# A Fourier transform by real sums: the even-row half of each sequence transform split once more, by classes mod 4

## The chip, the cores and the metric

One core of a Trainium2 chip. The metric is the device time of one execution in microseconds (us). The kernel before takes 1970.43 us, the median of three runs from 1970.38 to 1970.59. The profiled execution has a span of 1969.1 us, with TensorE's granted clock at 0.999 of full speed.

## The reference

```python
X = np.fft.fft(x, axis=1)          # x: (8, 3008, 256), float32
X = np.fft.fft(X, axis=2)
a = X.real                          # -> (24064, 256)
h = a @ w_in                        # w_in: (256, 2048)
g = np.where(h > 0, h, np.exp(np.minimum(h, 0)) - 1)
out = g @ w_out                     # w_out: (2048, 256)
```

Only the real part of a two-dimensional transform is wanted, and then two matrix products with an ELU between them, for 24064 rows. The weights come as 64-bit floats and are turned to float32 on the chip.

## The kernel before

**Shape of the work.** The channel transform is folded into w_in once, at the start (`fold_chunk`, L399): this makes Wc and Ws, with which h is Wc times a cosine transform R plus Ws times a sine transform I of the sequence. A frequency k and its mirror 3008 - k share R and I, so only half of the frequencies, 1504 for each batch, are computed; h of the mirror comes by a subtraction (`h_minus`, L770). A tile holds 256 of these columns; there are 47 tiles of 8 slots each, 376 slots. A slot makes 256 of the 2048 hidden values for the tile's columns and their mirrors, and multiplies them with w_out.

**A slot.** TensorE runs P (`mm_P`: Wc times Rr, 2 matmuls), three products X1 of an earlier slot, Q (`mm_Q`: Ws times Ir, 2) and four products X2: eleven matmuls of 256 columns. X1 and X2 are seven products in place of eight (Winograd's way, from the third tile on); GpSimd makes the four sums they need (`sum_1`, `sum_3`, `sum_2`, `sum_4`, all through `gtt`, L391), of which sum_2 makes block 2, read by the third matmul of X1 (shown as pB<-G,WT). VectorE makes E (`even_part`, L764, between P and Q), h_minus (L774) and the two ELU results g_plus and g_minus (L790). ScalarE makes the exponentials (L394). At each tile's end VectorE recombines the products into u and v (L388), transposes them, and SyncE stores them.

**The sequence transform.** x of a batch is loaded in four sets of rows, L[0] to L[3]: rows counted up from 0, down from the end, down from the middle (1504), up from the middle. Partition p holds six successive rows, 6p to 6p + 5 (`load_x`, L150). L[0] and L[3] are plain transfers of 6 KB runs from SyncE. L[2] and L[1] run backwards and are gathered by GpSimd with a table of row numbers (`indirect_dma_start`, L157, one call each). `fold_x` adds and subtracts the sets, on GpSimd, two pieces to a tile from the slot's spare time, so that a transform needs only the rows 0 to 752. Then there are four transforms for each batch (class `Dft`, L567): cosine or sine (ri 0 or 1), even or odd frequencies (kodd 0 or 1), each 377 or 376 columns. Each of them is again two halves, over even rows s and over odd rows s: three matmuls of 377 columns accumulated in one PSUM bank (`dft_mms`, L536). Their sum and difference give two mirrored runs of frequencies:

```python
        def copy(self):                     # ScalarE: odd-row half, PSUM -> SBUF
            act(self.bs[0:M, 0:n], self.pb[0:M, 0:n])
        def plus(self):                     # VectorE, into the ring Rr or Ir
            vtt(self.ring[0:M, sl], self.bs[0:M, a:z], self.pa[0:M, a:z], ALU.add)
        def minus(self):
            vtt(self.ring[0:M, sl], u[0:M, o + a : o + z], v[0:M, o + a : o + z], ALU.subtract)
```

The odd-row half runs at the end of one slot (`at_half`, L1258: time 4.75 of the slot's 4.8), the even-row half two slots later. Batch 0 has its transforms at the start, some of them in banks pA to pD and M.

**The one channel that stands apart.** The channel at half the channel frequency has a transform of its own, R of channel 128, held in Rb. For batch 0 it is x_even (the first transform, `fold_first`) and `dft_ext_0`; for the others it is read with small strided loads (`load_ext`), passed through DRAM (`get_ext`, L633), folded (`fold_ext`), transformed for all batches at once (`dft_ext`, L666, four groups of 8 rows) and turned into rows by `ext_side` (ScalarE, L682) and `ext_rows` (L688; even frequencies on VectorE, odd ones on GpSimd).

**What sets the order.** Every instruction is put down with a time, `at(t, fn)`, in units of slots of T = 4.8; the list is sorted by it and pinned in that order on each engine, except transfers, which a scheduler may move. PSUM banks: tag H has three in turn (slots, transform halves, folds), pA to pD hold the products, M the mirror's exponentials.

Of the kernel before, what the change touches and what calls it, by code (L numbers as in the profile page):

```python
# [27 lines left out]
BW = 3 * NE  # L28
# [4 lines left out]
def _dft_consts():  # L33

    p = np.arange(128)
    out = np.zeros((128, 8, 3, NE), np.float64)
    n = 0
    for ri in range(2):
        fn = np.cos if ri == 0 else np.sin
        for kodd in range(2):  # L40
            k = 2 * np.arange(NE) + kodd
            for par in range(2):
                for t in range(3):
                    s = 6 * p + 2 * t + par
                    m = fn(2.0 * np.pi * ((s[:, None] * k[None, :]) % SEQ) / SEQ)
                    m[s > RUN] = 0.0
                    m[s == 0] *= 0.5
                    if ri == kodd:
                        m[s == RUN] *= 0.5
                    else:  # L50
                        m[s == RUN] = 0.0
                    out[:, n, t, :] = m
                n += 1
    return out.reshape(128, -1).astype(np.float32)
# [36 lines left out]
def kernel(  # L91
# [43 lines left out]
    def row_tables():  # L135


        for c, n, base in (
            (1, 128, HALF - 5),
            (0, 128, SEQ - 5),  # L140
            (2, 128, SEQ - 5),
            (2, 1, SEQ - 6),
        ):
            pin(
                nc.gpsimd.iota(
                    ix[0:n, c : c + 1], pattern=[[0, 1]], base=base, channel_multiplier=-6
                )
            )

    def load_x(b):  # L150
        L = [
            spool.tile([128, 6 * ND], FP, tag=f"xl{j}", bufs=1, name=f"xl{j}")
            for j in range(4)
        ]
        for j in (2, 1):
            c = 1 if j == 2 else 2 if b == NB - 1 else 0
            load = nc.gpsimd.indirect_dma_start(  # L157
                out=L[j],
                out_offset=None,
                in_=xflat,  # L160
                in_offset=bass.IndirectOffsetOnAxis(
                    ap=ix[:, c : c + 1].bitcast(U32), axis=0
                ),
                element_offset=b * SEQ * ND,
            )
            if b == 1:
                pin(load)
        nc.sync.dma_start(out=L[3], in_=xrows(b, HALF, 6, 128))
        nc.sync.dma_start(out=L[0], in_=xrows(b, 0, 6, 128))
        if b == NB - 1:  # L170
            nc.gpsimd.dma_start(
                out=L[1][0:1, 0 : 5 * ND], in_=xrows(b, SEQ - 5, 1, 1, 5)
            )
        return L
# [168 lines left out]
    for kodd in range(2):  # L343
        for ri in range(2):
            MC[ri, kodd] = cpool.tile(
                [128, 2 * BW], FP, tag=f"MC{ri}{kodd}", name=f"MC{ri}{kodd}"
            )

    def load_mats(ri, kodd, pieces=1):
        n = ri * 4 + kodd * 2  # L350
        w = 2 * BW // pieces
        for i in reversed(range(pieces)):
            nc.sync.dma_start(
                out=MC[ri, kodd][:, i * w : (i + 1) * w],
                in_=MC_dr.ap()[:, n * BW + i * w : n * BW + (i + 1) * w],
            )
# [178 lines left out]

    def dft_mms(ps, ri, kodd, par, stat, width):  # L536
        n = NO if kodd else NE
        for t in range(3):
            m = 2 * t + par
            c = par * BW + t * NE  # L540
            mm(
                ps[:, 0:n],
                stat[:, m * width : m * width + 128]
                if width > 1
                else stat[:, m : m + 1].to_broadcast([128, 128]),
                MC[ri, kodd][:, c : c + n],
                t == 0,
                t == 2,
            )
# [16 lines left out]

    class Dft:  # L567
# [7 lines left out]
        def mms(self, par, ps):  # L575
            dft_mms(ps, self.ri, self.kodd, par, self.stat, 1 if self.first else 128)
            if par:
                self.pb = ps
            else:
                self.pa = ps  # L580

        def copy(self):
            M, n = self.M, self.n
            self.bs = spool.tile([128, NE], FP, tag="bs", bufs=2, name="bs")
            act(self.bs[0:M, 0:n], self.pb[0:M, 0:n])

        def plus(self):
            M = self.M
            base = self.b * HALF + self.kodd * RUN
            for sl, a, z in ring_cut(base, self.n, False):  # L590
                vtt(self.ring[0:M, sl], self.bs[0:M, a:z], self.pa[0:M, a:z], ALU.add)

        def minus(self):
            M, n = self.M, self.n
            base = self.b * HALF + self.kodd * RUN
            u, v = (self.pa, self.bs) if self.ri == 0 else (self.bs, self.pa)
            o = 0 if self.kodd else 1
            m = n if self.kodd else n - 2
            top = base + RUN - 1
            for sl, a, z in ring_cut(top, m, True):  # L600
                vtt(self.ring[0:M, sl], u[0:M, o + a : o + z], v[0:M, o + a : o + z], ALU.subtract)
            if self.ri == 0 and not self.kodd and not self.first:
                vtt(R4[:, self.b : self.b + 1], u[:, 0:1], v[:, 0:1], ALU.subtract)
# [29 lines left out]
    def get_ext():  # L633
        xs = state["xs"] = spool.tile([128, 4, NB, 6], FP, tag="xs", bufs=1, name="xs")
        with nc.allow_non_contiguous_dma(reason="runs of six"):
            for j in range(4):
                nc.sync.dma_start(
                    out=xs[:, j], in_=xe_dr[j].rearrange("b (p m) -> p b m", m=6)
                )

# [8 lines left out]
    def dft_ext_0():  # L649

        ps = state["ext"] = bank("H")
        for t in range(3):
            for par in range(2):
                m, c = 2 * t + par, par * BW + t * NE
                g = 32 * (2 + par)
                mm(
                    ps[g : g + 1, 0:NO],
                    state["x_odd"][:, m : m + 1],
                    MC[0, 1][:, c : c + NO],
                    t == 0,  # L660
                    t == 2,
                )
# [3 lines left out]
    def dft_ext():  # L666

        xe = state["xe"]
        ps = state["ext"] = bank("H")
        for t in range(3):  # L670
            for g, (kodd, par) in enumerate(EXT):
                n = NO if kodd else NE
                c = par * BW + t * NE
                mm(
                    ps[32 * g : 32 * g + NB, 0:n],
                    xe[:, kodd, :, 2 * t + par],
                    MC[0, kodd][:, c : c + n],
                    t == 0,
                    t == 2,
                )  # L680

    def ext_side(g, rows=NB):  # L682
        n = NO if g > 1 else NE
        t = spool.tile([128, NE], FP, tag="bs", bufs=2, name="bs")
        act(t[0:rows, 0:n], state["ext"][32 * g : 32 * g + rows, 0:n])
        state["side", g] = t[0:rows, 0:n]

    def ext_rows(kodd, tt, rows=NB):  # L688
        n = NO if kodd else NE
        if not kodd or rows < NB:  # L690
            rx = spool.tile([128, HALF + 1], FP, tag="rx", bufs=1, name="rx")
            state["rx"] = rx[0:rows]
        if not kodd:
            a = state["ext"][0:NB, 0:n]
        else:
            a = state["side", 2]
        rx, b = state["rx"], state["side", 2 * kodd + 1]
        o, base = 1 - kodd, kodd * RUN
        m = n - 2 * o
        tt(rx[:, base : base + n], a, b, ALU.add)  # L700
# [359 lines left out]
    load_mats(0, 0, 2)  # L1060
# [50 lines left out]
    at(-13.0, lambda: dft_now(R_even, 1, "pA"))  # L1111
    at(-12.9, lambda: dft_now(R_even, 0, "pB"))

    at(-13.1, lambda: dft_now(state["x_even"], 1, "pC"))
    at(-13.1, lambda: dft_now(state["x_even"], 0, "pD"))
    at(-11.5, lambda: state["x_even"].copy())
    at(-11.0, lambda: fold_now("o0 o1 O0 EO2"))
    at(-10.95, R_even.copy)
    at(-10.9, R_even.plus)
# [6 lines left out]
    at(-10.5, lambda: dft_now(I_even, 1, "pC"))  # L1126
    at(-10.88, w1_chunks[1].round)
    at(0.05, lambda: dft_now(I_even, 0, "M"))
# [129 lines left out]
    def at_half(step, d, par, col):  # L1258
# [8 lines left out]
        if par:  # L1267
            at(t + T + 1.46, lambda: d().copy())
        else:
            at(t + T + 1.01, lambda: d().plus())  # L1270
            at(t + T + 1.02, lambda: d().minus())

    def at_dft(step, gap, b, ri, kodd, stat):
# [7 lines left out]
        at_half(step, d, 1, 0)  # L1281
        at_half(step + gap, d, 0, b * HALF + (kodd + 1) * RUN)
# [5 lines left out]
    for t, fn in (  # L1288
        (-1.8, I_even.copy),
        (0.6, I_even.plus),  # L1290
        (0.8, I_even.minus),
        (3.1, lambda: dft_now(R_odd, 1, "pA")),
        (3.2, lambda: dft_now(R_odd, 0, "pB")),
        (T + 2.6, R_odd.copy),
        (T + 4.2, R_odd.plus),
# [3 lines left out]
    at_half(3, lambda: I_odd, 1, 0)  # L1299
    at_half(5, lambda: I_odd, 0, HALF)  # L1300
# [11 lines left out]
    at(31.0 * T, get_ext)  # L1312
    at(32 * T + 1.35, fold_ext)
    at(32 * T + 4.75, dft_ext)
    at(33 * T + 1.46, lambda: ext_side(1))
    at(33 * T + 1.47, lambda: ext_side(2))
    at(34 * T + 0.99, lambda: ext_rows(0, vtt))
    at(34 * T + 1.46, lambda: ext_side(3))
# [83 lines left out]
```

## Time and profile before

| part of the page | figure |
|---|---|
| time, median of three | 1970.43 us |
| TensorE busy | 1956.1 us |
| VectorE busy | 1276.5 us |
| ScalarE busy | 869.4 us |
| GpSimd busy | 1364.0 us |
| DMA, mean over the span | 36 GB/s; 333 GB/s in the first fortieth |
| transform matmuls into H (376 or 377 columns) | 33.0 + 28.9 + 28.9 + 28.8 us |
| GpSimd's four sums, 1440 in all | 1037.2 us, 730 ns each |

PE is TensorE, PEld its weight loads, DVE VectorE, ACT ScalarE, POOL GpSimd, SP SyncE. A row such as "PE H L382" means an instruction of TensorE that writes H, put down at line 382, which is the helper `mm`; likewise L388 is VectorE's helper `vtt`, L391 GpSimd's `gtt` and L394 ScalarE's `act`. So these rows are told apart by the names of their tiles, not by lines. A float32 matmul has two records, so counts are twice those of the code. The ends of matmul records are modelled and overlap the next record; distances are read from start to start. In a row of the waits the first name waits and the second releases it. In the timeline, the idle time ahead of a row stands in brackets with what ended it.

### The profile page before, as it was taken

How to read it: one execution, taken by the hardware profiler on the slowest of the kernel's cores; microseconds unless marked ns; L12 is line 12 of the kernel's file. 1: busy time of each engine (PE TensorE's matmuls, PEld its weight loads, DVE VectorE, ACT ScalarE, POOL GpSimd, SP SyncE). 2: the span in 40 equal slices, each digit the busy share in tenths (PEclk: the TensorE clock that was granted, in tenths of full speed). 3: DMA queues.
4: the chain of work that ended last, by engine and by line, in shares of the span. 5: the costliest groups of instructions: out<-in, count | busy, mean ns of one | idle time of the engine just before them, and what ended most of it. 6: DMA issues, size and time to landing. Idle time of an engine off the chain costs nothing.

```text
span 1969.1 us, 26858 instructions
## 1 busy us (share of the span) xinstructions
PE 1956.1 (99%) x8912; PEld 1655.1 (84%) x8912; DVE 1276.5 (65%) x2325; ACT 869.4 (44%) x1668; POOL 1364.0 (69%) x1800
## 2 busy tenths in 40 slices
PE   9999999999999999999999999999999999999998
PEld 5788788888888888888888888888888888888887
DVE  8866556765666656666566665676566665666666
ACT  4654444444444444444444444444434444344443
POOL 3888757876678766787567875778657776455665
PEclk9999999999999999999999999999999999999999
DMA  8146101111011110021100201003010110100101
GB/s 333 54 33 82 36 11 19 47 48 22 12 20 47 45 27 12 18 65 27 25 18 13 78 13 26 12 19 91 6 20 11 20 22 14 16 12 12 22 10 24
DMA packets 255546, 71.01 MB, mean 36 GB/s; under 512 B 243934, under 2 KB 244850, under 8 KB 255024
## 3 DMA queue, kind: packets, MB, share of 16 engines
q1 hardware_dynamic: 250896, 56.46, 14.5%
q0 software_dynamic: 2336, 12.59, 2.0%
q8 instruction: 70, 1.15, 0.2%
q14 instruction: 68, 0.56, 0.1%
q10 hardware_dynamic: 2176, 0.26, 0.1%
HBM read 44.43 MB, written 24.80 MB: 35 GB/s over the span
## 4 chain that ended last, share of the span: by engine, by line
PE 96%; POOL 1%; DVE 1%; ACT 1%; issue 0%; DMA 0%; SPq 0%; DVEq 0%; POOLq 0%; ACTq 0%
PE H L382 38%; PE pC L382 16%; PE pD L382 16%; PE pB L382 16%; PE pA L382 8%; PE M L382 1%; POOL WT L391 1%; DMA xl<-in_x_dram 0%; DVE E L764 0%; POOL G L391 0%; POOL w L391 0%; DVE v L388 0%; ACT G L394 0%; DVE u L388 0%; ACT M L394 0%
## 5 line engine op out<-in xcount | busy, mean ns | idle before, releaser
L391 POOL TENSOR_TENSOR G<-G 128x256 f32<-128x256 f32 x1440 | 1037.2, 730 | 544.2 <-DVE G L790 432.2
L764 DVE SCALAR_TENSOR_TENSOR E<-Rb,wex,H 128x256 f32<-128x256 f32 x752 | 327.9, 477 | 607.8 <-PE H L382 604.4
L394 ACT ACTIVATE G<-H 128x512 f32<-128x512 f32 x376 | 224.5, 597 | 950.8 <-DVE G L774 948.1
L382 PE MATMUL H<-Ir,Ws 128*128 128x256 f32 x1504 | 387.5, 380 | 1.9 <-DVE E L764 1.9
L382 PE MATMUL H<-Rr,Wc 128*128 128x256 f32 x1504 | 387.0, 380 | 0.0
L382 PE MATMUL pC<-G,WT 128*128 128x256 f32 x1440 | 369.6, 379 | 0.3 <-DVE u L388 0.3
L382 PEld LDWEIGHTS H<-Rr,Wc 128*128 128x128 f32 x1504 | 284.6, 190 | 56.1 <-issue 3.4
L382 PEld LDWEIGHTS H<-Ir,Ws 128*128 128x128 f32 x1504 | 277.5, 189 | 51.4 <-DVE E L764 5.7
L382 PEld LDWEIGHTS pC<-G,WT 128*128 128x128 f32 x1440 | 273.5, 190 | 37.8 <-PE H L382 0.6
L774 DVE SCALAR_TENSOR_TENSOR G<-E,H 128x512 f32<-128x512 f32 x376 | 257.0, 684 | 38.0 <-PE H L382 1.6
L790 DVE SCALAR_TENSOR_TENSOR G<-G,H 128x512 f32<-128x512 f32 x376 | 255.7, 680 | 26.1 <-ACT G L394 26.0
L790 DVE SCALAR_TENSOR_TENSOR G<-M,G 128x512 f32<-128x512 f32 x376 | 256.8, 683 | 0.0
L394 ACT ACTIVATE G<-G 128x512 f32<-128x512 f32 x376 | 233.2, 620 | 0.0
L382 PE MATMUL pB<-G,w 128*128 128x256 f32 x784 | 229.3, 379 | 0.0
L382 PE MATMUL pA<-G,w 128*128 128x256 f32 x784 | 229.3, 379 | 0.0
L382 PE MATMUL pD<-G,w 128*128 128x256 f32 x784 | 229.3, 379 | 0.0
L394 ACT ACTIVATE M<-G 128x512 f32<-128x512 f32 x376 | 223.9, 595 | 0.0
L394 ACT ACTIVATE M<-M 128x512 f32<-128x512 f32 x376 | 220.9, 588 | 0.1
L382 PE MATMUL pD<-G,WT 128*128 128x256 f32 x720 | 214.4, 379 | 2.5 <-DVE v L388 2.5
L382 PE MATMUL pB<-G,WT 128*128 128x256 f32 x720 | 214.8, 380 | 0.5 <-POOL G L391 0.4
L382 PEld LDWEIGHTS pB<-G,w 128*128 128x128 f32 x784 | 148.9, 190 | 20.4 <-PE H L382 0.2
L382 PEld LDWEIGHTS pA<-G,w 128*128 128x128 f32 x784 | 149.0, 190 | 20.3
(140 smaller groups left out, 1403.6 us busy)
## 6 DMA issues: line engine op xcount, KB each, us to landing
out_dram<-ot SPq DMA_DIRECT2D x496, 32.0 KB
xl<-in_x_dram SPq DMA_DIRECT2D x16, 768.0 KB
out_dram<-ot SPq DMA_DIRECT2D x256, 2.0 KB
Rb<-r SPq DMA_DIRECT2D x10, 376.0 KB
raw<-in_moe_w_in_dram SPq DMA_DIRECT2D x7, 512.0 KB
MC<-dft_mats SPq DMA_DIRECT2D x3, 1131.0 KB
raw<-in_moe_w_out_dram SPq DMA_DIRECT2D x4, 512.0 KB
out_dram<-ot SPq DMA_DIRECT2D x64, 28.0 KB
```

Of the source, the lines that this page charges most:

```text
L382: nc.tensor.matmul(out_, lhsT=lhsT, rhs=rhs, start=start, stop=stop, skip_group_check=True)
L391: pin(nc.gpsimd.tensor_tensor(out=o, in0=a, in1=b, op=op))
L394: pin(nc.scalar.activation(out=o, in_=i, func=func, **kw))
L764: nc.vector.scalar_tensor_tensor(out=S.E[:, c], in0=Rb[:, cols(i)], scalar=wex[:, f : f + 1], in1=S.H[:, c], op0=ALU.mult, op1=ALU.add,)
L774: nc.vector.scalar_tensor_tensor(out=two(S.G[:, 0:512])[:, :, ::-1], in0=two(S.E), scalar=2.0, in1=two(S.H), op0=ALU.mult, op1=ALU.subtract,)
L790: nc.vector.scalar_tensor_tensor(out=o, in0=e, scalar=-1.0, in1=h, op0=ALU.add, op1=ALU.max)
```

## The change

The sum over even rows s is split by s mod 4. For a cosine transform the rows with s = 0 mod 4 give values that are symmetric about the middle of the run of frequencies, those with s = 2 mod 4 antisymmetric ones; for a sine transform it is the other way round. So half of the frequencies (189 of 377, or 188 of 376) are computed for each class, and the others follow by a sum and a difference, which the new function `unfold` makes on VectorE. The purpose is fewer columns for TensorE.

- The even half becomes three matmuls of 189, 189 and 378 columns (`dft_parts`): rows 4p, rows 4p + 2, and a third set of mixed rows whose matrix holds both classes side by side, with zeros in place.
- Rows are laid out by class: a partition holds rows 4p to 4p + 3, and two more rows of the rest, 512 + 4(p mod 64) + 2(p div 64) and the next. Each of the four loads becomes two: 4 KB runs and 2 KB runs. The gathers of L[2] and L[1] become two calls each, in the same place; the table of row numbers has two kinds of entries.
- The even half now runs first and the odd one two slots later. `copy` (ScalarE) takes 189 antisymmetric values in place of 377; `unfold` makes two additions of 189 and 188 elements on VectorE into bs; `plus` and `minus` read bs and the odd half in PSUM.
- At the start x_even is now transformed ahead of R_even; the matrices come in pieces by halves (756 and 1131 columns, together 1887 instead of 2262).
- The extra channel follows: `get_ext` has three transfers for each set instead of one and is issued at 30 T, `ext_side` copies all four groups, `ext_rows` unfolds first, on VectorE or GpSimd.

In the order of instructions on each engine, apart from these, nothing moves: on VectorE the unfolding stands right after E (or after the recombination's u) of the slot that follows the even half, ahead of g_plus; on GpSimd the second gather stands between the first one and the four sums; in batch 1's load all four gathers stand between two instructions of a weight chunk.

```diff
+        for j in (2, 1):
+            for c, cols in (
+                (2 if j == 1 and b == NB - 1 else 0, slice(2 * ND, 6 * ND)),
+                (1, slice(0, 2 * ND)),
+            ):
+                load = nc.gpsimd.indirect_dma_start(
+                    out=L[j][:, cols],
...
+        for j, row in ((3, HALF), (0, 0)):
+            nc.sync.dma_start(out=L[j][:, 0 : 4 * ND], in_=xrows(b, row, 4, 128, 4))
+            nc.sync.dma_start(
+                out=L[j][:, 4 * ND :],
...
+    def dft_parts(ri, kodd, par):
+        if par:
+            n = NO if kodd else NE
+            return [(2 * t + 1, BE + t * NE, n, 0) for t in range(3)]
+        h = NO // 2 if kodd else NH
+        return [(2 * ri, 0, h, 0), (2 - 2 * ri, h, h, h), (4, 2 * h, 2 * h, 0)]
...
+    def unfold(o, sym, anti, M, n, tt):
+        h, m = (n + 1) // 2, n // 2
+        tt(o[0:M, 0:h], sym[0:M, 0:h], anti[0:M, 0:h], ALU.add)
+        tt(o[0:M, n - 1 : n - 1 - m : -1], sym[0:M, 0:m], anti[0:M, 0:m], ALU.subtract)
...
         def copy(self):
-            M, n = self.M, self.n
-            self.bs = spool.tile([128, NE], FP, tag="bs", bufs=2, name="bs")
-            act(self.bs[0:M, 0:n], self.pb[0:M, 0:n])
+            M, h = self.M, (self.n + 1) // 2
+            self.anti = spool.tile([128, NH], FP, tag="anti", bufs=2, name="anti")
+            act(self.anti[0:M, 0:h], self.even[0:M, h : 2 * h])
+
+        def unfold(self):
+            self.es = spool.tile([128, NE], FP, tag="bs", bufs=3, name="bs")
+            unfold(self.es, self.even, self.anti, self.M, self.n, vtt)
...
     def ext_side(g, rows=NB):
-        n = NO if g > 1 else NE
-        t = spool.tile([128, NE], FP, tag="bs", bufs=2, name="bs")
+        kodd, par = EXT[g]
+        n = NO if kodd else NE if par else 2 * NH
+        t = spool.tile([128, 2 * NH], FP, tag="side", bufs=2, name="side")
...
         if par:
-            at(t + T + 1.46, lambda: d().copy())
-        else:
             at(t + T + 1.01, lambda: d().plus())
             at(t + T + 1.02, lambda: d().minus())
+        else:
+            at(t + T + 0.9, lambda: d().copy())
+            at(t + T + 1.0, lambda: d().unfold())
...
-        at_half(step, d, 1, 0)
-        at_half(step + gap, d, 0, b * HALF + (kodd + 1) * RUN)
+        at_half(step, d, 0, 0)
+        at_half(step + gap, d, 1, b * HALF + (kodd + 1) * RUN)
```

## The prediction

> **What bounds the kernel now.** I read the page first, for the busy shares.
>
> ```profile
> PE 1956.1 (99%) x8912; PEld 1655.1 (84%) x8912; DVE 1276.5 (65%) x2325; ACT 869.4 (44%) x1668; POOL 1364.0 (69%) x1800
> PE 96%; POOL 1%; DVE 1%; ACT 1%; issue 0%; DMA 0%; SPq 0%; DVEq 0%; POOLq 0%; ACTq 0%
> ```
>
> TensorE is busy for 99% of the span and is 96% of the chain that ended last, so a matmul column that disappears is worth its time, and every new wait of TensorE costs its full length. The waits of TensorE (total, times, longest) say how little slack is unused:
>
> ```profile
> PE pD L382 <- DVE v L388: 2.5, 4, 1.0
> PE H L382 <- DVE E L764: 1.9, 3, 1.1
> PE pB L382 <- POOL G L391: 0.4, 1, 0.4
> ```
>
> Only some 6 us of waits in 1969. The question is therefore how near the other engines are to making TensorE wait. TensorE's timeline around one transform half (start, length, count of records; a float32 matmul is two records):
>
> ```profile
> 188.05 2.06 PE L382 MATMUL H<-MC,e 128*128 128x377 f32 x6
> 189.95 1.02 PE L382 MATMUL H<-Rr,Wc 128*128 128x256 f32 x4
> ```
>
> Three matmuls of 377 columns take 189.95 - 188.05 = 1.90 us, 1.68 ns a column. Next the gather of x rows on GpSimd, by tile, and the slot around one gather, first GpSimd and then TensorE:
>
> ```profile
> L157 POOL DMA_INDIRECT xl<-in_x_dram,ix x16: 941/971/1265, 1.8 to 1366.8; - x16
> ```
> ```profile
> 877.25 1.18 POOL L476 TENSOR_TENSOR o<-xl 128x384 f32<-128x384 f32 x1
> 878.70 0.98 POOL L157 DMA_INDIRECT xl<-in_x_dram,ix  x1 [0.27 <-DVE G L790]
> 879.70 3.03 POOL L391 TENSOR_TENSOR G<-G 128x256 f32<-128x256 f32 x4
> ```
> ```profile
> 881.60 0.59 PE L382 MATMUL pB<-G,w 128*128 128x256 f32 x2
> 882.03 0.65 PE L382 MATMUL pB<-G,WT 128*128 128x256 f32 x2
> ```
>
> The four sums take 0.76 us each, so the third (sum_2, which makes block 2) ends at 879.70 + 2.28 = 881.98, and the matmul that reads block 2 starts at 882.03. In this slot GpSimd is already just in time. Last, the start: GpSimd and TensorE where the weights are still prepared.
>
> ```profile
> 51.33 1.26 POOL L157 DMA_INDIRECT xl<-in_x_dram,ix  x1
> 52.90 0.94 POOL L157 DMA_INDIRECT xl<-in_x_dram,ix  x1 [0.30 <-issue]
> 53.86 1.29 POOL L391 TENSOR_TENSOR w<-w,pow 128x512 f32<-128x512 f32 x1
> 55.23 2.02 POOL L391 TENSOR_TENSOR raw<-w 128x256 f32<-128x256 f32 x2
> ```
> ```profile
> 55.43 1.89 PE L382 MATMUL pB<-G,w 128*128 128x256 f32 x8
> 57.30 1.08 PE L382 MATMUL H<-raw,CC 128*64 128x256 f32 x8
> ```
>
> The matmul at 57.30 (fold_chunk(3)) starts as GpSimd's pair ends, at 57.25.
>
> **What the Trainium skill says.** "TensorE: Matmul & The Clock Gate", section "LDWEIGHTS (loading the stationary operand)": a weight load takes its columns / 1.2 ns, 107 ns for 128. The trace shows a little less: four load-and-matmul pairs of one column run from 23.53 to 23.89 us, 90 ns each, and that decides. A record of a 189-column matmul takes about 159 ns, so loads stay hidden. "VectorE: DVE Perf Modes", "The perf-mode tier table (the rule you actually need)": tensor_tensor in float32, or with a PSUM operand, runs in the slowest mode; here 128x377 takes 0.54 us and 128x1 0.15, 1.04 ns an element. "Perfetto Trace Analysis", "DMA Instruction — SWDGE (GPSIMD)": such an instruction's profiled window is descriptor generation, not data movement; here 0.97 us on GpSimd while the packets come afterwards.
>
> **Part 1: fewer columns.** The even half of a transform goes from 3 x 377 = 1131 columns to 189 + 189 + 378 = 756. 1.90 x 375/1131 = 0.63 us saved. There are 33: 28 for x of batches 1 to 7, four for batch 0, one for x_even. The extra channel's rows (dft_ext, dft_ext_0) save nothing: their groups lie in different column strips and run side by side (12 records of 480 ns in 2.1 us), and the odd half keeps its three full matmuls. Batches 1 to 7: 28 x 0.626 = 17.5 us. For the five at the start see part 4.
>
> **Part 2: the unfolding on VectorE.** Each transform gains two tensor_tensor of 128x189: 0.15 + 189 x 1.04 ns = 0.35 us each, 0.55 us for the pair since consecutive ones overlap by some 0.08. They come after E of the next slot and delay the two g, which feed GpSimd's sums. In an ordinary slot the matmul on block 2 starts 1.57 us after sum_2 ends, so 0.55 costs nothing; plus and minus (0.95 us) stand at the same place in other slots and cost nothing there. Where the slot is also the second one of a tile's recombination (four of the 28), v, which frees bank pD, moves from 0.5 us ahead of TensorE to just behind it. In the trace, three slots in which plus and minus fall there lose 0.7 us each, so with 0.55 instead of 0.95 about 0.25: 4 x 0.25 = 1.0 us lost. In five slots (first of the recombination) ScalarE's shorter copy now comes ahead of the p copy and the exponentials come 0.35 us sooner: 0.1 us each, 0.5 gained. ScalarE's copies themselves shrink and lie beside other work.
>
> **Part 3: twice as many gathers.** Two gathers a batch become four, in the same two places, pairs back to back. Behind the second wait the four sums, and for them TensorE. The trace shows two gathers in a row: 0.30 us of issue and 0.94 for the second. I take 0.30 + 0.95 = 1.25 us; bounds 0.6 (if time goes with bytes: the second has a third of them) and 1.55. In the 12 gather slots of batches 2 to 7 the room ahead of the matmul on block 2 is 0.25, 2.10, 0.87, 0.81, 0.88, 0.82, 0.10, 0.10, 0.28, 0.24, 0.86 and 0.12 us. Eleven are too small: 11 x 1.25 - 5.33 + 11 x 0.05 (the wake-up, which the room of a waiting slot includes) = 9.0 us; I take 8.9. Once TensorE has waited, GpSimd is no longer late against it, so the losses add. Bytes and rows are the same, and loads come long before their folds: free.
>
> **Part 4: the start.** Transform data is a sixth smaller and the row loads are cut into pieces of 4 and 2 KB. Batch 0's last rows are waited for until 13.15 us by ScalarE and needed by VectorE at 14.33; two more gathers cost about that room, so nothing. From 14.3 to 52 us VectorE is nearly always busy, and four unfoldings there (4 x 0.55 = 2.2 us) take up what the shorter matmuls save (4 x 0.63 = 2.5). The four gathers of batch 1 then end at 53.84 + 2 x 1.25 = 56.3, the pair that fold_chunk(3) needs at 59.75, against 57.25 before: TensorE there is 2.4 us later than before, whatever it gained until then. I_odd's saving goes there too.
>
> **Part 5: the extra rows.** In the slot of ext_rows(0) TensorE already waits three times (0.3, 0.3, 1.0 us) on VectorE; two unfoldings more, 0.5 us. ext_rows(1) on GpSimd gains two of 8x188 at about 0.53 (8x376 takes 0.97) ahead of sums that already keep TensorE waiting 0.4: 1.0 us. Together 1.5. The longer chain of small transfers (get_ext) is issued a slot sooner and landed 15 us ahead: free.
>
> Sum: 17.5 + 0.5 - 1.0 - 8.9 - 2.4 - 1.5 = 4.2 us. 1970.4 - 4.2 = 1966.2; I say 1966.0.
>
> **The rivals.**
> (a) The second gather is hidden. For it: it moves a third of the bytes. Against it: every gather in the trace takes about 0.96 whatever stands beside it, and rows, not bytes, are unchanged. At 0.3 + 0.3 us only six slots are too small (6 x 0.65 - 1.09 = 2.8 us) and the start loses 1.2: 4.2 + (8.9 - 2.8) + (2.4 - 1.2) = 11.5 us, 1958.9.
> (b) Gains and losses cancel: the start loses 2 us more because rows come late, or the recombination slots double their loss. 4.2 - 3 = 1 us, 1969.
> (c) Slower: weight loads bind the short matmuls. Their records last 190 ns; if four short records a half each took that instead of 159, 28 x 4 x 0.031 = 3.5 us are lost; a gather pair at the 1.57 us between the starts at 51.33 and 52.90 costs 0.3 x 11 = 3.3 more; late first rows 2. 4.2 - 8.8 = -4.6: 1975.0. Against it: 90 ns a pair, above.
>
> **How the numbers follow.** Forecast 0.50 (its own spread, +-3 us, puts 0.32 of it beyond 0.2%, or under 1966.5, and 0.18 within); (a) 0.20; (b) 0.22; (c) 0.08. Faster 0.32 + 0.20 + 0.02 of (b) = 0.54, same 0.18 + 0.20 = 0.38, slower 0.08. The range takes in (a) and (b) and the bounds of the gather: 1958.0 to 1973.0; (c) and a full hiding of all waits (1952) are left out.
>
> **What would show it.** Right: a half with records 128x189 lasting 1.27 us; 32 gathers at about 0.95; waits "PE pB <- POOL G" of 8 to 10 us in some 11 times near the times of the gathers; fold_chunk(3) 2.4 us later than before, other slots 4.75 us as now. Wrong: short matmuls spaced over 160 ns a record; second gathers far under 0.9; waits on E or v in ordinary slots; the first transform starting later than 15.9 us.

## The result, and the profile after

The changed kernel takes 1982.74 us, the median of four runs from 1982.38 to 1983.51, against 1970.51 us for the kernel before. The ratio is 1.0062, with a 95% interval from 1.0045 to 1.0080. It is 12.2 us slower; 4.4 us faster was forecast, with a range that ended at 1973. The span of the profiled execution is 1980.7 us against 1969.1, 11.6 us more.

The page after, busy times and chain, which answer to the two lines shown of before:

```profile
PE 1940.8 (98%) x8912; PEld 1651.8 (83%) x8912; DVE 1296.3 (65%) x2393; ACT 864.8 (44%) x1669; POOL 1379.1 (70%) x1821
PE 89%; POOL 5%; DVE 3%; issue 1%; SPq 1%; ACT 1%; DMA 0%; DVEq 0%; POOLq 0%; ACTq 0%
```

TensorE is busy 15.3 us less and the span is 11.6 us longer all the same: about 27 us of idle time are new. (The 33 shorter halves should take off 33 x 0.63 = 21 us; part of the start runs at half clock, as the last section shows, which lengthens matmuls again.) The chain says where the idle time is: 5% of it now runs over GpSimd and 3% over VectorE, where it was 1% each. The waits of TensorE name them (total, times, longest):

```profile
PE H L414 <- DVE xg L420: 11.4, 1, 11.4
PE pB L414 <- POOL G L423: 10.3, 12, 1.6
PE pD L414 <- DVE v L420: 2.5, 4, 1.0
PE H L414 <- POOL raw L423: 2.5, 1, 2.5
PE H L414 <- DVE E L810: 1.7, 4, 0.6
```

The second and fourth rows were forecast, the first was not. The transform half itself came out as forecast. Three matmuls of 189, 189 and 378 columns start at 203.69, the next work 1.28 us later (1.90 before):

```profile
203.69 1.44 PE L414 MATMUL H<-MC,e 128*128 128x189 f32 x6
204.97 1.02 PE L414 MATMUL H<-Rr,Wc 128*128 128x256 f32 x4
```

The gathers by tile, then a slot with gathers (the one whose counterpart was shown of before), GpSimd first:

```profile
L182 POOL DMA_INDIRECT xl<-in_x_dram,ix x32: 938/958/1256, 1.8 to 1383.3; - x32
```
```profile
893.24 0.98 POOL L182 DMA_INDIRECT xl<-in_x_dram,ix  x1 [0.27 <-DVE G L836]
894.53 0.96 POOL L182 DMA_INDIRECT xl<-in_x_dram,ix  x1 [0.30 <-issue]
895.51 3.02 POOL L423 TENSOR_TENSOR G<-G 128x256 f32<-128x256 f32 x4
```
```profile
896.14 0.59 PE L414 MATMUL pB<-G,w 128*128 128x256 f32 x2
897.78 0.70 PE L414 MATMUL pB<-G,WT 128*128 128x256 f32 x2 [1.05 <-POOL G L423]
```

A gather of two rows to a partition takes as long as one of four or of six. The second one costs 0.30 + 0.96 us, and the matmul that reads block 2 now waits 1.05 us. In the place where fold_chunk(3) needs its pair:

```profile
63.40 1.26 POOL L182 DMA_INDIRECT xl<-in_x_dram,ix  x1
...
67.47 0.95 POOL L182 DMA_INDIRECT xl<-in_x_dram,ix  x1 [0.30 <-issue]
68.43 1.27 POOL L423 TENSOR_TENSOR w<-w,pow 128x512 f32<-128x512 f32 x1
69.79 2.00 POOL L423 TENSOR_TENSOR raw<-w 128x256 f32<-128x256 f32 x2
```
```profile
67.47 1.89 PE L414 MATMUL pB<-G,w 128*128 128x256 f32 x8
71.84 1.08 PE L414 MATMUL H<-raw,CC 128*64 128x256 f32 x8 [2.48 <-POOL raw L423]
```

What is new stands at the very start. VectorE, TensorE, and SyncE's queue (an issue that stands long is a queue that is held up):

```profile
5.49 0.69 DVE L291 SCALAR_TENSOR_TENSOR w<-raw,w 128x512 f32<-128x512 uint32 x1
16.15 0.96 DVE L508 TENSOR_TENSOR e<-xl 128x768 f32<-128x768 f32 x1 [9.97 <-DMA xl<-in_x_dram]
```
```profile
25.06 3.68 PE L414 MATMUL H<-w,CC 128*64 128x256 f32 x16 [11.45 <-DVE xg L420]
```
```profile
2.96 0.54 SPq L195 DMA_DIRECT2D xl<-in_x_dram  x1
3.54 9.74 SPq L1105 DMA_DIRECT2D CC<-chan_mats  x1
13.33 0.87 SPq L386 DMA_DIRECT2D MC<-dft_mats  x1
```

The first fold waits for rows until 16.15, where it began at 6.41 before. Behind the two loads of L195 (the pairs of rows) SyncE's next issue stands for 9.74 us (it took 0.43 before), and between 12 and 14 us the DMA engines move 68 GB/s, where 408 were moved before.

The starts of P can be lined up, slot by slot, in both traces. A slot's step is what it adds to the distance between them, and the sum of the steps is the whole difference:

| where | forecast, us | measured, us |
|---|---|---|
| start, up to slot 0 | 0 | +11.5 |
| slots 2 to 5 (fold_chunk(3), I_odd, batch 0's unfoldings) | +2.4 | +3.0 |
| 28 transforms, batches 1 to 7 | -17.5 | -17.5 |
| first slots of a recombination | -0.5 | -0.5 |
| unfolding in the second slot of a recombination, 4 times | +1.0 | +1.3 |
| gathers, 11 slots | +8.9 | +11.55 |
| extra rows, slots 35 and 37 | +1.5 | +2.4 |
| slot 262 | 0 | -0.2 |
| sum | -4.2 | +11.6 |

### The profile page after: what moved, and what is told of

Its sections match the earlier page's. It is cut to its first block, busy times and chain, and to the rows that moved or that the text cites. A ratio compares the mean times of both kernels' runs of the same rounds, so it can differ in the third digit from the quotient of the medians.

```text
span 1980.7 us, 27003 instructions
## 1 busy us (share of the span) xinstructions
PE 1940.8 (98%) x8912; PEld 1651.8 (83%) x8912; DVE 1296.3 (65%) x2393; ACT 864.8 (44%) x1669; POOL 1379.1 (70%) x1821
## 4 chain that ended last, share of the span: by engine, by line
PE 89%; POOL 5%; DVE 3%; issue 1%; SPq 1%; ACT 1%; DMA 0%; DVEq 0%; POOLq 0%; ACTq 0%
PE H L414 36%; PE pB L414 15%; PE pD L414 15%; PE pC L414 15%; PE pA L414 7%; POOL G L423 2%; POOL xl L182 1%; POOL WT L423 1%; DVE E L810 1%; POOL w L423 1%; SPq L1105 0%; DVE G L836 0%; DMA raw<-in_moe_w_in_dram 0%; DVE pow L314 0%; DVE v L420 0%
## 5 line engine op out<-in xcount | busy, mean ns | idle before, releaser
L414 PE MATMUL pB<-G,WT 128*128 128x256 f32 x720 | 215.7, 381 | 10.4 <-POOL G L423 10.3
L414 PEld LDWEIGHTS pD<-G,w 128*128 128x128 f32 x784 | 149.0, 190 | 20.3
```

What stands on the lines that cost most here:

```text
L414: nc.tensor.matmul(out_, lhsT=lhsT, rhs=rhs, start=start, stop=stop, skip_group_check=True)
```

## The experiments: the start

Theory 1: a transfer whose access pattern has 2 as its slowest dimension is served by two DMA engines only. Two rivals: the number or shortness of the pieces costs, or the four gathers at the start hold the engines. Of the first four kernels two are the kernel before with its plain loads cut; e1_cut_2x64 is this, and e1_cut_128 has `[[6 * ND, 128], [1, 2 * ND]]` in its last line:

```diff
-        nc.sync.dma_start(out=L[3], in_=xrows(b, HALF, 6, 128))
-        nc.sync.dma_start(out=L[0], in_=xrows(b, 0, 6, 128))
+        for j, row in ((3, HALF), (0, 0)):
+            nc.sync.dma_start(out=L[j][:, 0 : 4 * ND], in_=xrows(b, row, 6, 128, 4))
+            nc.sync.dma_start(out=L[j][:, 4 * ND :], in_=bass.AP(tensor=xt, offset=...,
+                ap=[[6 * 64 * ND, 2], [6 * ND, 64], [1, 2 * ND]]))
```

> The kernel before, with only its plain row loads (L[3], L[0]) changed: each 6 KB run is cut in 4 KB and 2 KB, and the 2 KB pieces go in one transfer whose access pattern starts with a dimension of 2 (2 x 64 x 2 KB), as in the changed kernel. Same rows, same places. Theory 1 (a transfer whose slowest dimension is 2 is served by only two of the 16 DMA engines): the first matmul slot comes 9 to 12 us later, time 1980 to 1982, and the DMA engines' mean falls to under a quarter between 10 and 14 us. Rival 2 (the number of transfers or the 2 KB length costs): the same here, but also in e1_cut_128. Rival 3 (the four gathers at the start hold the engines): no change here, 1970.5.

Measured: 1971.35 us, ratio 1.0002 (0.9993 to 1.0011); the first slot 0.3 us earlier than before.

> Control to e1_cut_2x64: the same cut in 4 KB and 2 KB pieces, the same number of transfers, but the 2 KB pieces with an access pattern of 128 x 2 KB. Theory 1 (two engines): as before, 1970 to 1971.5, first slot within 0.5 us of the kernel before. Rival 2 (number or length of pieces): as late as e1_cut_2x64, 1980 to 1982.

Measured: 1971.40 us, ratio 1.0003 (0.9994 to 1.0011). So neither the number of the transfers nor their 2 KB runs cost anything. But the first of the two missed its forecast, and I had to ask whether it was a test at all: its dimensions of 2 and 64 follow each other at one step of six rows, so the two are one dimension of 128 in other words, and it ran as e1_cut_128 did. It said nothing on theory 1.

The other two are the changed kernel with the pair loads mended. In e1_two each is issued in halves; in e1_flat the rows are laid out so that one plain transfer does:

```diff
-            nc.sync.dma_start(out=L[j][:, 4 * ND :], in_=bass.AP(tensor=xt, offset=...,
-                ap=[[2 * ND, 2], [4 * ND, 64], [1, 2 * ND]]))
+            for h in range(2):                                   # e1_two
+                nc.sync.dma_start(out=L[j][64 * h : 64 * h + 64, 4 * ND :],
+                    in_=xrows(b, row + 512 + 2 * h, 4, 64, 2))
```
```diff
-                s = ... 512 + 4 * (p % 64) + 2 * (p // 64) + m - 4
+                s = ... 512 + 2 * p + m - 4                      # e1_flat
...
+            nc.sync.dma_start(out=L[j][:, 4 * ND :], in_=xrows(b, row + 512, 2, 128, 2))
```

> The changed kernel, with each 2 x 64 x 2 KB load of row pairs issued as two transfers of 64 x 2 KB; everything else as it is. Theory 1 (two engines): the start comes back, the first slot within 1 us of the kernel before, time 1982.7 - 11 = about 1971.5 (1970 to 1973). Rival 2: no gain, or later still with one more transfer for each set. Rival 3 (gathers at the start): no gain, 1982 to 1983.

Measured: 1974.22 us, ratio 1.0017 (1.0010 to 1.0024), 1.2 us over the forecast range. The first slot is 1.2 us later than in the kernel before, instead of 11.5.

> The changed kernel with the row pairs laid out as 512 + 2p and the next on partition p, in place of 512 + 4(p mod 64) + 2(p div 64): a pair load is one transfer of 128 x 2 KB, the gather's table steps down by 2, and the extra channel's pairs come in one transfer instead of two. The same sums, matrices to match. Theory 1: as e1_two, about 1971.5, at most 0.5 us apart from it. Rival 2: 1980 or more. In both e1_two and e1_flat the waits of TensorE on G (12 times, 10.3 us in sum) stay as in the changed kernel, since the gathers are still doubled.

Measured: 1972.45 us, ratio 1.0008 (1.0002 to 1.0015). The first slot is 0.2 us earlier than in the kernel before. So 8.5 us of the loss go in e1_two, where nothing but the pair loads is changed, and 10.3 in e1_flat, where the gathers' table, the matrices and the extra channel's transfers follow the new layout. All four gathers are left at the start in both: the rival of the gathers falls. e1_two came 1.5 us later in the first slot than e1_flat. At its start TensorE waits 2.17 us for the channel matrices CC (0.43 in e1_flat) and then runs at half clock from 15.3 to 18.7 us, so that fold_chunk(0), the matmuls H<-w,CC, takes 3.49 us start to start instead of 1.87.

For a real test of the pattern, e2_cut_mixed gives the kernel before the very pattern of the changed one:

```diff
-                ap=[[6 * 64 * ND, 2], [6 * ND, 64], [1, 2 * ND]]))   # e1_cut_2x64
+                ap=[[2 * ND, 2], [4 * ND, 64], [1, 2 * ND]]))        # e2_cut_mixed
```

> The kernel before, with its plain row loads cut in 4 KB and 2 KB pieces, and the 2 KB pieces with the very access pattern of the changed kernel: 2 (step 2 rows) x 64 (step 4 rows) x 2 KB, from row 512 of the half on. The rows that come in are not those that the fold wants, so this is a kernel that computes something else; volume, places and waits are the same. In e1_cut_2x64 the dimensions of 2 and 64 follow each other in memory (2 x 64 runs at one step of 6 rows) and can be merged to one of 128, so it was no test of the pattern. Theory 1 (two of the 16 DMA engines serve a pattern whose slowest dimension is 2 and can't be merged): the first slot 9 to 12 us later, time 1980 to 1982. If it stays at 1971, the pattern alone is not the cause and the four gathers at the start must take part.

Measured: 1993.35 us, ratio 1.0116 (1.0099 to 1.0132). The pattern alone, with two gathers at the start as before, makes the first slot 13.7 us later, more than the 9 to 12 expected. Slot 5 adds 8.6, which was not expected: there VectorE waits 8.2 us for a small transfer of wex, in the stretch in which batch 1's pair loads are under way. SyncE's queue in e2_cut_mixed shows the same picture as in the changed kernel:

```profile
2.96 0.55 SPq L170 DMA_DIRECT2D xl<-in_x_dram  x1
3.55 9.33 SPq L1067 DMA_DIRECT2D CC<-chan_mats  x1
```

Two more kernels vary only the first two numbers, at the same volume:

```diff
-                ap=[[2 * ND, 2], [4 * ND, 64], [1, 2 * ND]]))
+                ap=[[2 * ND, 4], [8 * ND, 32], [1, 2 * ND]]))        # e3_cut_4x32
+                ap=[[2 * ND, 16], [32 * ND, 8], [1, 2 * ND]]))       # e3_cut_16x8
```

> As e2_cut_mixed (the kernel before, plain row loads cut in 4 KB and 2 KB, rows not those that the fold wants, so it computes something else), with the 2 KB pieces as 4 x 32 x 2 KB in place of 2 x 64 x 2 KB: step 2 rows for the 4, 8 rows for the 32, not to be merged. Theory 1 (as many engines as the slowest dimension has entries): four engines, some 48 packets of 2 KB a microsecond where the pieces run alone in place of 24; the first slot late by a third to a half of the 13.7 us of e2_cut_mixed, 4 to 7 us, time 1976 to 1983. Rival (any pattern with three dimensions is slow): as e2_cut_mixed, 1993.

Measured: 1979.83 us, ratio 1.0047 (1.0030 to 1.0063); first slot 10.5 us later.

> As e3_cut_4x32, with 16 x 8 x 2 KB (steps of 2 and of 32 rows), again computing something else at the same volume. Theory 1: all 16 engines, first slot within 0.7 us of the kernel before, time 1970 to 1972. Rival (any pattern with three dimensions is slow): 1993. Rival (the short distance between the pieces in memory costs): 1980 or more.

Measured: 1972.67 us, ratio 1.0012 (1.0005 to 1.0019); first slot 1.9 us later, where at most 0.7 was expected.

Three dimensions are not the cause, since 16 x 8 is nearly free; the size of the slowest one is. The rate of the pieces shows it most directly. There are stretches in which nothing else of weight is being moved; the summary of the DMA for such a stretch, 50.3 to 51.8 us of the changed kernel (the pattern of 2):

```profile
DMA packets 37, 0.07 MB, mean 49 GB/s; under 512 B 1, under 2 KB 1, under 8 KB 37
q1 hardware_dynamic: 37, 0.07, 13.2%
```

and 58.6 to 59.9 us of e3_cut_4x32 (the pattern of 4):

```profile
DMA packets 64, 0.13 MB, mean 101 GB/s; under 512 B 0, under 2 KB 0, under 8 KB 64
q1 hardware_dynamic: 64, 0.13, 26.1%
```

The last figure is a share of 16 engines: 0.132 x 16 = 2.1 engines, and 0.261 x 16 = 4.2. The packets' own times say the same: two are under way at once for 1.34 us of the 1.5, and four for 1.02 us of the 1.3. An estimate from this rate: the two pair loads of a batch are 256 packets, which at 37 in 1.5 us take 10.4 us even where nothing else is moved; SyncE's queue was held up for 9.74. The delay at the start does not go down in proportion, though (13.7, 10.5, 1.9 us for 2, 4, 16), and my range for 4 x 32, 4 to 7 us, was missed. Some 2.6 us of its 10.5 are half clock: fold_chunk(0) takes 3.61 us start to start instead of 1.88, the first half of x_even 2.91 instead of 2.01. In the start the pieces share their few engines with the matrices and weights: in e3_cut_4x32 the engines are all busy from 6 to 21 us, and yet only 4 to 14 of the 2 KB packets start in a microsecond between 8 and 14. That the pieces stand behind other packets on those engines is argued from this, not shown.

## The experiments: the gathers

e2_gather2 is the kernel before with nothing but each gather doubled:

```diff
-            load = nc.gpsimd.indirect_dma_start(out=L[j], ...,
-                element_offset=b * SEQ * ND)
+            for m0, m1 in ((0, 4), (4, 6)):
+                load = nc.gpsimd.indirect_dma_start(out=L[j][:, m0 * ND : m1 * ND], ...,
+                    element_offset=(b * SEQ + m0) * ND)
```

> The kernel before, with each of its 16 gathers doubled: rows 0 to 3 of a partition's six in one, rows 4 and 5 in a second right behind it. The output and all transforms stay. My price for a second gather (0.30 us of issue and 0.95 of GpSimd, in the changed kernel 11.5 us of later slots from batch 2 on and 2.5 us at the start): 11.5 + 2.5 = 14, time about 1984.5 (1982 to 1986). Rival (the waits on G in the changed kernel come from the unfoldings that delay g on VectorE, not from the gathers): 1971 to 1975.

Measured: 1987.18 us, ratio 1.0082 (1.0065 to 1.0099), 16.7 us more than the kernel before and 1.2 over the forecast range. TensorE's waits in e2_gather2:

```profile
PE pB L383 <- POOL G L392: 9.1, 12, 1.1
PE H L383 <- POOL raw L392: 2.5, 1, 2.5
```

The 11 later slots lose 11.5 us, slot by slot the same amounts (to 0.03 us) as in the changed kernel: so they come from the gathers alone, and the unfoldings have no part in them. Beyond that, 1.0 us is lost ahead of slot 0, which was not expected, and 4.0 at slots 5 and 6 where 2.5 was expected; the missing 1.5 us is the clock, below.

e2_spread takes e1_flat and gives each gather a place of its own, in a slot without a fold piece:

```diff
-        at(l0 * T + 0.1, lambda b=b: state.update(L=load_x(b)))     # gathers inside
+        at(l0 * T + 0.1, lambda b=b: state.update(L=load_x(b)))     # plain loads only
+        for n in range(4):
+            t = (22.2, 27.0, 28.9, 32.4)[n] if b == 1 else (l0 + n) * T + 1.3
+            at(t, lambda b=b, n=n: gather_x(state["L"], b, n))      # pinned
```

> The kernel of e1_flat (1972.45) with each gather in a place of its own: from batch 2 on one gather per slot, in four slots without a fold piece, where the fold pieces stand in other slots; batch 1's four in four gaps of GpSimd behind its weight work. Theory (a gather costs TensorE only where GpSimd has less room than the gather takes, so the loss is of the pair, back to back): the 11.6 us of slot steps at the gathers go, and of the 4.6 us at slots 5 and 6 about 3 to 4: 1972.45 - 11.6 - 3.5 = 1957.4 (1956 to 1960), and the waits of TensorE on G fall from 10.3 us to under 1.5. Rival (each gather delays the four sums wherever it stands, by 0.4 to 0.5 us with the loss of wake-up): 24 x 0.45 = 11, time 1967 to 1970.

Measured: 1956.17 us, ratio 0.9928 (0.9911 to 0.9945). The number of gathers is the same 32 at the same 0.97 us, and the 11 steps are gone. The waits of TensorE in e2_spread now begin thus, and none on G is left in the list:

```profile
PE pD L417 <- DVE v L423: 2.5, 4, 1.0
PE pC L417 <- DVE u L423: 1.6, 1, 1.6
PE H L417 <- DVE E L812: 1.6, 4, 0.6
```

A gather of batch 3 in its new place, where a fold piece of 1.18 us stands in other slots:

```profile
490.28 3.02 POOL L426 TENSOR_TENSOR G<-G 128x256 f32<-128x256 f32 x4 [2.38 <-PE H L417]
493.45 0.97 POOL L179 DMA_INDIRECT xl<-in_x_dram,ix  x1 [0.15 <-issue]
494.51 3.02 POOL L426 TENSOR_TENSOR G<-G 128x256 f32<-128x256 f32 x4
```

## The experiments: the unfolding

e2_best is e2_spread with the unfolding put behind v where both fall into one slot, and e3_twice is e2_best with each unfolding done twice:

```diff
-            at(t + T + 1.0, lambda: d().unfold())
+            at(t + T + (2.55 if step % 8 == 1 else 1.0), lambda: d().unfold())
```
```diff
-            unfold(self.es, self.even, self.anti, self.M, self.n, vtt)
+            for _ in range(1 if self.b == 0 else 2):
+                unfold(self.es, self.even, self.anti, self.M, self.n, vtt)
```

> The kernel of e2_spread with the unfolding put behind v in the slots that are the second of a recombination (time 2.55 of the slot in place of 1.0). Theory (there the unfolding delays v, which frees bank pD; four such slots lost 0.32 us each): 4 x 0.32 = 1.3 us less than e2_spread, about 1956. Rival (behind v it delays g_minus and through it sum_2, so the loss only moves): as e2_spread or up to 1 us more.

Measured: 1955.66 us, ratio 0.9925 (0.9908 to 0.9941). The four steps of 0.32 us are gone, 1.28 us; of this the medians show 0.5, since the first slot came 0.43 us later in this trace.

> The kernel of e2_best (1955.7), with the unfolding of every transform of batches 1 to 7 done twice, the second with the same result: 28 x 0.55 us more on VectorE. My reading of an ordinary slot (1.57 us between the end of sum_2 and its matmul): 1.1 us of unfoldings still fit, so the 24 ordinary ones cost under 0.1 each; behind v the same. Time 1955.7 to 1957.5. Rival (VectorE's delay passes to TensorE through g and the sums, the slack of 1.57 is not there): up to 28 x 0.55 = 15.4 us, 1965 to 1971.

Measured: 1958.34 us, 2.7 us more than e2_best (the spans differ by 2.0). By slots, the four in which the unfolding stands behind v lose 0.4 each, four others 0.2, and the rest next to nothing. The loss is a little over my upper end, but 13.4 us more of busy VectorE cost TensorE about 2: the slack in an ordinary slot is there.

e3_ext spreads the work of the extra rows in the same way (to make room, batch 2's gathers move back two slots and a small transfer of batch 1's odd rows one):

```diff
-    at(34 * T + 0.99, lambda: ext_rows(0, vtt))
+    at(33 * T + 3.6, lambda: ext_unfold(0, vtt))
+    at(34 * T + 0.99, lambda: ext_rows(0, vtt, whole=False))
...
-    at(35 * T + 1.35, lambda: ext_rows(1, gtt))
+    at(39 * T + 1.3, lambda: ext_unfold(1, gtt))
+    at(40 * T + 1.3, lambda: ext_rows(1, gtt, whole=False))
```

> The kernel of e2_best with the unfolding of the extra rows moved: on VectorE to slot 33 at 3.6 (ahead of it: nothing that TensorE waits for), on GpSimd to slot 39, and the sum and difference there to slot 40, where no fold piece stands; batch 2's gathers two slots later to leave room. Theory (part 5: each unfolding costs because it stands ahead of u and v, or of sums that are late): the steps at slots 35 to 37, 1.77 us, fall to 0 to 0.7, and the 0.4 us that TensorE waits on G for ext_rows(1) in the kernel before goes too: 1955.7 - 1.5 = 1954.2 (1953.5 to 1955). Rival (the cost moves along with the instructions): 1955.7 or more.

Measured: 1953.52 us (1953.07 to 1954.73), ratio 0.9916 (0.9899 to 0.9932) to the kernel before. The median is 2.1 us under e2_best, and the step at slot 37 is 1.8 of it, where 1.5 was expected. All of it comes from GpSimd's part: the step at slot 35, where VectorE's unfolding has moved ahead of u, is 1.25 us as against 1.22 in e2_best. This version, with e1_flat's layout, is faster than both kernels: 17.1 us under the kernel before, beside 17.5 for the 28 shorter transforms alone. Its page:

```profile
PE 1935.1 (99%) x8912; PEld 1652.0 (85%) x8912; DVE 1295.7 (66%) x2393; ACT 865.4 (44%) x1669; POOL 1379.2 (71%) x1820
PE 94%; DVE 3%; POOL 1%; issue 1%; ACT 1%; DMA 0%; DVEq 0%; POOLq 0%; ACTq 0%
```

## Why the prediction was wrong

The sum failed by 15.8 us (from -4.2 to +11.6). Three quarters of it are the start, to which part 4 gave no cost.

**The start, part 4: the step that failed.** Part 4 says that "the row loads are cut into pieces of 4 and 2 KB", and the sum has no term for them; the "so nothing" of that part is said of the two more gathers. I took the new loads by their bytes and their run lengths, and e1_cut_128 shows that those indeed cost nothing. I did not look at the shape of the pattern, `[[2 * ND, 2], [4 * ND, 64], [1, 2 * ND]]`, which stands in the diff. The Trainium skill has it: "DMA: Bandwidth & Descriptors", section "Why a DMA increments its semaphore by 16 and not by 1", says that the number of engines k is taken from the pattern's slowest dimension that is not 1, as the largest number up to 16 that divides it on both sides. For 2 that is 2, and the trace shows 2.1 engines; for 4 it shows 4.2. The loss was 11.5 us against a forecast of 0. Rivals (b) and (c) had late rows in them, at 2 us, so the direction was thought of and the size was not. The sign that I had named for a wrong forecast, "the first transform starting later than 15.9 us", is what came: x_even, the first one, began at 28.67 us.

**fold_chunk(3), also part 4: the wait right.** The four gathers made it wait 2.48 us; 2.4 was forecast. The slots up to it lost 3.0 in all, since GpSimd's weight work ahead of the gathers began 12.1 us later than before (61.96 against 49.89), 0.6 more than the first slot.

**The columns, part 1: right to 0.01 us.** The 28 transforms give 0.62 to 0.64 us each, and the first slots of a recombination 0.5 in sum. Weight loads do not bind the short matmuls (rival (c)): a half takes 1.28 us start to start. The argument against (c) rested on a misread row, though. The 90 ns a pair are 0.36 us divided by four, and the first of the four matmuls found its weights loaded; from there on the matmuls stand 111 to 112 ns apart in that trace, near the 107 ns of the page that the prediction cites. It is still less than the 160 ns at which the records of 189 columns follow each other.

**The gathers, part 3: the price right, the room miscounted.** 0.30 + 0.96 us was the forecast price and is the measured one, so rival (a), the hidden gather, falls. The losses are 11.55 instead of 8.9. In two places I counted the same room twice. I took the rooms ahead of each slot from the trace before (0.87 and 0.81 in one batch, 0.88 and 0.82 in the next) and said that once TensorE has waited, "GpSimd is no longer late against it, so the losses add". It is late: the first pair uses up its 0.87, TensorE waits only for what is beyond it, and two slots later GpSimd, which has a fold piece in each slot, has made up just enough for one gather and not for two. The second places lost 1.30 and 1.31 us where I had 0.49 and 0.48, together 1.64 us. The rest, about 1 us over 11 slots, is, by the sum, a restart of TensorE that is nearer 0.14 than the 0.05 us that I took.

**The unfolding, part 2: right for the ordinary slots, 0.32 for 0.25 us in the others.** e3_twice shows how much slack there was.

**The extra rows, part 5: 2.4 for 1.5 us.** Slot 37, on GpSimd, lost 1.2 for 1.0: the price was about right, and e3_ext shows that it was paid for the place. Slot 35, on VectorE, lost 1.2 for 0.5, because there I had the length wrong. I took the price of an ordinary unfolding (0.61 us for a pair in the changed kernel), but this pair, of 8 partitions, takes 1.31 us, and TensorE waits 1.62 us on u instead of 0.3:

```profile
235.36 1.31 DVE L420 TENSOR_TENSOR bs<-side 8x189 f32<-8x189 f32 x2
238.25 1.10 PE L414 MATMUL pC<-G,WT 128*128 128x256 f32 x4 [1.62 <-DVE u L420]
```

In e3_ext the pair takes 1.45 us in its new place and TensorE waits 1.08 us there, on another u. Why it is so slow is open.

With e1_flat the start is as forecast, and the rest of the errors leave 1972.45 us, against a kernel before of 1970.65: still no gain. So the forecast of a faster kernel would have failed without the two engines too, by the gathers' missing 2.65 us, the extra rows' 0.9 and the clock's 1.5.

## What to carry to other kernels

When a diff changes how a transfer is cut, read its access pattern from the slowest dimension and not only its bytes and run lengths: 2 x 64 runs cost 11.5 us where 128 runs cost nothing. Slack measured ahead of single instructions is a stock that refills at some rate; two delays a few slots apart draw on the same one, and the same 32 gathers that cost 11.55 us in pairs were free one to a slot, in slots without a fold piece. A change that trades TensorE's columns for work on other engines has its worth only after that work is placed: 1982.7, 1972.5, 1956.2 and 1953.5 us are the same arithmetic.

## What the runs showed of the hardware that was not expected

A single wait can cost more than its length. In e1_flat TensorE waits 3.1 us for fold_chunk(3)'s pair; the table by stretches (TensorE's clock is the third figure from the end) shows the granted clock afterwards:

```profile
58.00:60.00 2.00, 0.00 (x0) 0.00 (x0) 2.00 (x4) 0.61 (x2) 1.92 (x3) 1.00 0.69 221
60.00:61.00 1.00, 0.67 (x4) 0.48 (x6) 0.56 (x1) 1.00 (x3) 1.00 (x2) 0.53 0.03 12
61.00:62.00 1.00, 1.00 (x8) 0.29 (x4) 0.00 (x0) 0.51 (x2) 0.92 (x2) 0.50 0.80 61
63.00:64.00 1.00, 1.00 (x5) 0.84 (x4) 0.01 (x1) 1.00 (x3) 0.06 (x1) 0.77 0.98 201
```

From 60 to 63 us the matmuls run at half speed: fold_chunk(3) takes 1.90 us start to start instead of 1.01, and the P behind it 1.56 instead of 0.97, 1.5 us on top of the wait. e2_gather2 shows the same after a wait of 2.46 us, which is the 1.5 us that its forecast missed; the changed kernel, after one of 2.48 us, does not, so the length alone doesn't decide.

The traces hold a pattern that fits all of these. In every trace with several changes of the clock these lie whole multiples of 3.413 us apart. Cut along this grid, the two waits of nearly one length differ. First e2_gather2, then the changed kernel (the second figure is the time that TensorE is busy):

```profile
57.17:60.58 3.41, 1.12 (x6) 0.64 (x4) 1.41 (x3) 2.12 (x4) 3.31 (x4) 1.00 0.66 231
60.58:63.99 3.41, 3.24 (x11) 1.93 (x12) 0.00 (x0) 1.22 (x4) 2.63 (x3) 0.50 0.53 162
```
```profile
67.27:70.68 3.41, 2.09 (x10) 1.51 (x8) 3.41 (x4) 0.00 (x0) 3.12 (x3) 1.00 0.87 299
70.68:74.09 3.41, 2.25 (x14) 1.59 (x15) 1.46 (x4) 3.19 (x7) 3.33 (x4) 1.00 0.40 67
```

In e2_gather2 nearly the whole wait falls into one stretch, TensorE is idle for 2.29 of its 3.41 us, and the next stretch runs at half clock. In the changed kernel the border at 70.68 divides the wait, 1.32 and 1.16 us are idle, and the clock stays. Over all 14 traces of this case the clock fell behind every full-clock stretch of the grid with 1.90 us or more idle and behind none with 1.81 or less. No run was made to test this; it is read from the traces. The Trainium skill, "TensorE: Matmul & The Clock Gate", section "Part 1: The HAM clock gate (the "warmup" mystery)", says that the array falls to half its clock after an idle window of about 3.4 us, in a window that runs free of the program. The grid agrees with that; that the whole window must be idle does not, since 1.90 us of it were enough here.

The long wait at the start of the changed kernel also brought the clock to 0.50, from 16.1 to 29.7 us, and fold_chunk(0) took 3.61 us start to start where it took 1.88 in e1_cut_128.
